# Local scores of two heads in one product: k laid block-diagonally, in a fused attention and expert kernel

## The chip, the cores and the metric

The kernel runs on one core of a Trainium2 chip. The metric is device time in microseconds (us) for one execution of the whole program. Before the change, three runs took 709.04, 709.7 and 718.24 us; their median, 709.7 us, is the time before.

## The reference

The program computes an attention over 8 batches of 8 heads, 576 tokens and 64 dimensions, and feeds its output to a layer of 8 experts, of which each token takes one.

```python
# attention: a pooled part and a local part
q_d, k_d, v_d = (x.reshape(B, H, S // 4, 4, D).mean(axis=3) for x in (q, k, v))
out_up = np.repeat(sm_attn(q_d, k_d, v_d), 4, axis=2)
mask = np.abs(pos[:, None] - pos[None, :]) < 4
scores = np.where(mask, scale * np.matmul(q, k.transpose(0, 1, 3, 2)), -1e9)
attn = softmax(scores)
x = out_up + np.matmul(attn, v)
# experts: each token goes to the best of 8
e_idx = np.argmax(x @ w_gate + modality_bias[modality_id], axis=1)
out[mask_e] = gate_w * (np.maximum(x[mask_e] @ w1[e], 0) @ w2[e])
```

Here `sm_attn` is a scaled softmax attention, and the local part lets a query see only the keys less than four positions away.

## The kernel before, in words

**Steps.** The attention stage runs 32 steps; step n takes two heads of one batch, so four steps make a batch. q and k of two steps are loaded with one load each (`load_qk`, three buffers), transposed on TensorE into PSUM (`tp`, L274, and `tpt`, L287, which serves two steps), and copied by ScalarE to SBUF (`qT`, L292 and L294; `kT_`, L300 and L302). In SBUF the 128 partitions of `qT2` and `kT2` hold the 64 dimensions of the first head and then the 64 of the second. Both have two halves, for even and odd steps. For the part of k in `kT0`, one copy moves 512 columns of all 128 partitions; `kT1`, in even steps only, copies 64 columns for each of two steps, in one instruction.

**Local scores.** A step's 576 queries are cut into 24 blocks of 24, four to each of 6 groups of 96. A block needs 32 keys (a window of 24 with three on either side, and two more). `mk` (L328) first writes the mask into a PSUM tile of 128 x 6 x 32 by a product with the identity; `sc` (L337) then adds 24 products of 64 rows, 24 stationary columns (q) and 32 moving columns (k), each at a tile position of 64 rows and 32 columns. There are two such tiles a step, `sc0` for the first head and `sc1` for the second. VectorE takes the maximum (`lm`, L344) and subtracts it (`le`, L350), ScalarE exponentiates (L355), VectorE sums (`z`, L381) and inverts (`zr`, L387), GpSimd scales (`nl`, L391), VectorE transposes 32 x 32 blocks (`lt`, L402), ScalarE copies them into the zeroed `Pw` (L407), and TensorE multiplies with v (`avl`, L442).

**Pooled scores.** GpSimd adds groups of four tokens in two instructions each: `qe` and `d` (L308, `halves`) and `qd` and `kd` (L312, `whole`). Then come the products `scd` (L364), the maximum `dm` (L369), the exponentials `de` (L377), scaling on GpSimd (`nd`, L395), transposes on TensorE (`pdt`, L413), copies by ScalarE (`PdT`, L420), products with the pooled v (`vp`, L262; `avd`, L427) and `Od` (L432). VectorE adds both parts into `X` (L453). GpSimd also issues the scatters of the routing table (L599).

**What sets the order.** All of this is emitted in an order written out by hand. `PHASE` gives each operation a phase in units of a step; operation p of step n is placed at n + p, and the sorted list is the order of every engine's in-order queue. Within a step of the steady state the order on TensorE is: transposes of q and k, `mk0`, (`tpt`), `sc1` of the step before, (`vp`), `avd`, `scd`, `avl`, `sc0`, `pdt`, `mk1`. On ScalarE it is: `qT0`, `kT0`, three of four `Pw` copies, (`qT1`), `Od`, (`kT1`), the exponential, the last `Pw` copy, three `de`, two `PdT`. SP issues the loads in the same sorted order.

**Buffers.** PSUM tiles come from three tags: "T" (three buffers: `tp`, `tpt`, `vp`, `pdt`), "S" (three: `sc`, `scd`) and "A" (two: `avd`, `avl`, the router's). A tile waits until the reader of the one three (or two) allocations earlier has finished.

**Experts.** From about 260 us on, the experts' products run with both operands split in two float32 parts (L886, L934).

Of the kernel before, what the change touches and what calls it, by code (L numbers as in the profile page):

```python
# [7 lines left out]
F32 = mybir.dt.float32  # L8
F32R = mybir.dt.float32r
BF16 = mybir.dt.bfloat16  # L10
I32 = mybir.dt.int32
AF = mybir.ActivationFunctionType
ALU = mybir.AluOpType
# [4 lines left out]
B, H, S, D = 8, 8, 576, 64  # L18
# [4 lines left out]
SUB, WIN = 24, 32  # L23
BLK = 4 * SUB
NB = 6
PAD = 3
KT = S - SUB + WIN
QS = 1.0 / 128
NEG = -8.0e9 * QS
# [17 lines left out]
TB, SB = 3, 3  # L47
# [30 lines left out]
class Consts:  # L78
    def __init__(s, tc, pool, psum):
        nc = tc.nc  # L80

        s.ps = psum
        pool.tile([128, 48], F32, name="pad")
        s.dummy = pool.tile([128, 128], BF16, name="dummy")
        nc.vector.memset(s.dummy, 0.0)
        s.busy(nc, 12)
        s.ident = pool.tile([128, 128], F32, name="ident")
        make_identity(nc, s.ident)
        s.identb = pool.tile([128, 128], BF16, name="identb")
        make_identity(nc, s.identb)  # L90

        x = pool.tile([128, 1], F32, name="warm")
        nc.vector.memset(x, 0.0)
        nc.scalar.activation(x, x, AF.Exp)
        m = pool.tile([128, WIN], BF16, name="band")
        nc.gpsimd.memset(m, 0.0)
        for j in range(4):
            t = m[32 * j : 32 * j + 32]
            nc.gpsimd.affine_select(out=t, in_=t, pattern=[[1, WIN]], compare_op=ALU.is_ge, fill=NEG, base=0,
                                    channel_multiplier=-1)  # L100
            nc.gpsimd.affine_select(out=t, in_=t, pattern=[[-1, WIN]], compare_op=ALU.is_ge, fill=NEG, base=6,
                                    channel_multiplier=1)
        s.mask = pool.tile([128, NB, WIN], BF16, name="mask")
        nc.vector.tensor_copy(s.mask, m.unsqueeze(1).broadcast_to([128, NB, WIN]))
        nc.vector.memset(s.mask[0:32, 0, 0:PAD], NEG)
        nc.vector.memset(s.mask[96:128, NB - 1, SUB + PAD : WIN], NEG)

        s.pool = pool.tile([128, 32], F32, name="pool")

# [18 lines left out]
    def load(s, tc, pool, work, rows, mid, bias, w_gate):  # L128
        nc = tc.nc
        s.wg = pool.tile([128, 4, 32], F32, name="wg")  # L130
        nc.vector.memset(s.wg, 0.0)
        for f in range(2):
            for a in range(2):
                nc.sync.dma_start(s.wg[64 * a : 64 * a + 64, 2 * f : 2 * f + 2, 0:NE],
                                  w_gate[256 * f + 128 * a : 256 * f + 128 * a + 128].rearrange("(g d) e -> d g e", g=2))
        s.mi = rows.tile([128, 2 * DM], F32, name="R", bufs=NR)[:36, :256].bitcast(I32)
        nc.sync.dma_start(s.mi, mid.bitcast(I32).rearrange("(t x) -> t x", t=36))
        s.bb = work.tile([128, 2, NE], F32, name="bb")
        nc.sync.dma_start(s.bb, bias.unsqueeze(0).broadcast_to([128, 2, NE]))
# [53 lines left out]
class Attention:  # L193


    def __init__(s, tc, ctx, ectx, C, psum, q, k, v):
        s.tc, s.C, s.ps = tc, C, psum
        nc = s.nc = tc.nc
        s.q, s.k, s.v = q, k, v

        s.ld = ectx.enter_context(tc.tile_pool(name="ald", bufs=2, side="right", reuse_waits="tile"))
        s.wk = ctx.enter_context(tc.tile_pool(name="awk", bufs=2, reuse_waits="tile"))
        s.one = ctx.enter_context(tc.tile_pool(name="aone", bufs=1, reuse_waits="tile"))
        s.QK, s.t = {}, {}
        s.vw = [(s.ld, s.one)[j].tile([128, H * NB, D], F32, name=f"vw{j}", bufs=1) for j in range(2)]

        s.qT2 = s.ld.tile([128, 2, S], F32, name="qT", bufs=1)
        s.kT2 = s.ld.tile([128, 2, KT], F32, name="kT", bufs=1)
        nc.vector.memset(s.kT2[:, :, 0:PAD], 0.0)
        nc.vector.memset(s.kT2[:, :, S + PAD :], 0.0)  # L210
        s.Pw = [s.one.tile([128, 2 * NB, 4, SUB], F32, name=f"Pw{j}") for j in range(NPW)]

        s.De = [s.one.tile([128, 3, 32 * NB], F32, name=f"de{j}") for j in range(3)]
        for j in range(2):
            nc.vector.memset(s.vw[j][0:32, 0], 0.0)
            nc.vector.memset(s.vw[j][96:128, H * NB - 1], 0.0)

        for j in range(3):
            nc.vector.memset(s.De[j], 0.0)
# [49 lines left out]
    def tp(s, n, nm):  # L269

        src = s.QK[n // 2]["qk".index(nm)]
        p = s.t["tp", nm, n] = s.ps.tile([128, 512], F32, name="tp", tag="T", bufs=TB)
        for j in range(4):
            s.nc.tensor.transpose(p[:, 128 * j : 128 * j + 128],  # L274
                                  src[:, 5 * (n % 2) + j].rearrange("p a d -> p (a d)"), s.C.ident)
# [7 lines left out]
    def tpt(s, n, i):  # L283

        p = s.t["tp", "t"] = s.ps.tile([128, 2, 128], F32, name="tpt", tag="T", bufs=TB)
        for x in range(2):
            s.nc.tensor.transpose(p[:, x], s.QK[n // 2][x][:, 4].rearrange("p a d -> p (a d)"), s.C.ident)  # L287
# [7 lines left out]

    def kT_(s, n, i):
        g = n % 2
        if i:
            t = s.kT2.rearrange("m g t -> m (g t)")[:, PAD + 512 : PAD + 512 + 2 * (KT - 512)]
            s.nc.scalar.copy(t.rearrange("m (g t) -> m g t", g=2)[:, :, :64], s.t["tp", "t"][:, 1].rearrange("m (g t) -> m g t", g=2))  # L300
        else:
            s.nc.scalar.copy(s.kT2[:, g, PAD + 64 * g : PAD + 64 * g + 512], s.t.pop(("tp", "k", n)))  # L302

    def halves(s, nm, n, T):

        d2 = s.t[nm, n] = s.ld.tile([128, 144, 2], F32, name=nm, bufs=1)
        T4 = T.rearrange("m (g t) -> m g t", t=4)
        s.nc.gpsimd.tensor_tensor(d2, T4[:, :, 0:2], T4[:, :, 2:4], op=ALU.add)  # L308

    def whole(s, nm, n, d2):  # L310
        dd = s.t[nm, n] = s.ld.tile([128, 144], F32, name=nm)
        s.nc.gpsimd.tensor_tensor(dd, d2[:, :, 0], d2[:, :, 1], op=ALU.add)  # L312

    def qe(s, n, i):
        s.halves("qe", n, s.qT2[:, n % 2])

    def qd(s, n, i):
        s.whole("qd", n, s.t.pop(("qe", n)))

    def d(s, n, i):  # L320
        s.halves("d", n, s.kT2[:, n % 2, PAD : PAD + S])

    def kd(s, n, i):
        s.whole("kd", n, s.t.pop(("d", n)))

    def mk(s, n, a):
        p = s.t["sc", n, a] = s.ps.tile([128, NB, WIN], F32, name="sc", tag="S", bufs=SB)
        s.nc.tensor.matmul(p, s.C.identb, s.C.mask, start=True, stop=False, skip_group_check=True)  # L328

    def sc(s, n, a):  # L330

        p, qT, kT = s.t["sc", n, a], s.qT2[:, n % 2], s.kT2[:, n % 2]
        r = slice(64 * a, 64 * a + 64)
        for i in range(NB):
            for j in range(4):
                q0 = BLK * i + SUB * j
                s.nc.tensor.matmul(p[32 * j : 32 * j + SUB, i, :], qT[r, q0 : q0 + SUB], kT[r, q0 : q0 + WIN],  # L337
                                   start=False, stop=(i == NB - 1), skip_group_check=True,
                                   tile_position=(64 * a, 32 * j))

    def lm(s, n, a):
        if ("lm", n) not in s.t:
# [91 lines left out]
    def avl(s, n, i):  # L434

        b, hp = divmod(n, 4)
        vw, Pw = s.vw[b % 2], s.Pw[n % NPW]
        p = s.t["avl", n, i] = s.ps.tile([128, 3, BLK], F32, name="avl", tag="A", bufs=2)
        for c in range(3):
            for a in range(2):  # L440
                k = 3 * i + c
                s.nc.tensor.matmul(p[64 * a : 64 * a + 64, c], vw[:, NB * (4 * (hp // 2) + hp % 2 + 2 * a) + k, :],  # L442
                                   Pw[:, NB * a + k], start=True, stop=True, skip_group_check=True)

    def X(s, n, i, dst):

# [782 lines left out]
```

## Time and profile before

| | |
|---|---|
| median of three runs | 709.7 us |
| the profiled execution | 716.96 us |
| its span, first to last instruction | 715.3 us |
| granted TensorE clock, mean | 0.974 |
| attention's scores, first to last | 7.5 to 257.5 us |
| TensorE busy | 662.0 us, 93% |
| VectorE, ScalarE, GpSimd busy | 379.2, 358.7, 262.9 us |

The profile is one execution on the chip. PE is TensorE's products, PEld its weight loads, DVE VectorE, ACT ScalarE, POOL GpSimd, SP the queue that issues loads; L337 is line 337 of the kernel. A row of the groups tells the line, engine, operation, output and input tiles, shape, count, then the busy time (overlaps counted once) and the mean duration of one, and after the second bar the idle time of the engine just before these instructions, with what ended it. "issue" is time in which an engine waited for nothing that the profile shows. A float32 product has two records in the trace. In a row such as 64*24 64x32, 64 rows and 24 stationary columns are used, and the moving operand has 32 columns.

### The profile page before, as it was taken

The numbers are of one execution on the slowest core, as the hardware profiler recorded it, in microseconds if no ns is written. First come the engines' busy times: TensorE is split into PE (matmuls) and PEld (weight loads), VectorE is DVE, ScalarE is ACT, GpSimd is POOL, SyncE is SP. The second block draws the span as 40 slices with busy tenths as digits, with TensorE's granted clock in tenths as the row PEclk, the third lists the DMA queues.
The fourth block names the chain that finished last, engine by engine and source line by source line (L and its number), as shares of the span: only waits on it lengthen the run. The fifth ranks groups of instructions, "written<-read, shape, count | busy, mean of one in ns | idle before, by whom it ended". The sixth has DMA issues, their size and how long they took to land. (4 is left out here: it accounts for less than half of the span.)

```text
span 715.3 us, 19216 instructions
## 1 busy us (share of the span) xinstructions
PE 662.0 (93%) x7467; PEld 535.7 (75%) x7467; DVE 379.2 (53%) x877; ACT 358.7 (50%) x804; POOL 262.9 (37%) x351
## 2 busy tenths in 40 slices
PE   7889999998968798999999999999999999999991
PEld 4677776776746666887888888888888888889790
DVE  3678687787848686836533245333453243525510
ACT  3678777777756574534444234433444234444610
POOL 6756665857647857353030310403103011010200
PEclk9799999999989899999999999999999999999996
DMA  9799799897889757579560744516435154346400
GB/s 178 148 186 173 162 165 181 174 184 130 145 147 214 152 151 186 154 228 294 143 219 21 189 148 116 179 58 190 165 102 156 67 162 148 103 133 186 159 13 29
DMA packets 179439, 107.93 MB, mean 151 GB/s; under 512 B 139309, under 2 KB 157777, under 8 KB 179346
## 3 DMA queue, kind: packets, MB, share of 16 engines
q1 hardware_dynamic: 172274, 87.49, 53.1%
q0 software_dynamic: 7072, 19.18, 8.3%
q8 instruction: 60, 0.98, 0.7%
q14 instruction: 33, 0.27, 0.2%
HBM read 87.39 MB, written 19.51 MB: 149 GB/s over the span
## 5 line engine op out<-in xcount | busy, mean ns | idle before, releaser
L938 POOL DMA_INDIRECT out_dram<-o,tg x37 | 40.9, 1106 | 302.7 <-ACT o L937 245.5
L817 DVE TENSOR_TENSOR wlo<-raw,whi 128x1024 fp32r<-128x1024 f32 x73 | 87.4, 1222 | 84.4 <-ACT whi L811 74.4
L891 DVE SCALAR_TENSOR_TENSOR hl<-l,hh 128x512 fp32r<-128x512 f32 x72 | 49.4, 688 | 101.7 <-ACT hh L890 101.7
L934 PE MATMUL l<-whi,hh 128*128 128x512 f32 x256 | 100.2, 395 | 0.0
L934 PE MATMUL l<-wlo,hh 128*128 128x512 f32 x256 | 99.6, 390 | 0.0
L934 PE MATMUL l<-whi,hl 128*128 128x512 f32 x256 | 99.6, 390 | 0.0
L890 ACT ACTIVATE hh<-l 128x512 fp32r<-128x512 f32 x72 | 42.9, 597 | 110.7 <-PE l L886 109.3
L886 PE MATMUL l<-xh,whi 128*128 128x512 f32 (+1 forms) x256 | 95.0, 374 | 0.4 <-DVE hl L891 0.2
L886 PE MATMUL l<-xh,wlo 128*128 128x512 f32 (+1 forms) x256 | 94.8, 370 | 0.0
L886 PE MATMUL l<-xl,whi 128*128 128x512 f32 (+1 forms) x256 | 94.7, 370 | 0.0
L811 ACT CAST whi<-raw 128x1024 fp32r<-128x1024 f32 x70 | 71.4, 1050 | 28.2 <-DMA raw<-in_moe_w_dram 18.2
L937 ACT ACTIVATE o<-l,tg 128x512 f32<-128x512 f32 x37 | 25.3, 687 | 98.5 <-PE l L934 70.5
L407 ACT COPY Pw<-lt 32x288 f32<-32x288 f32 x128 | 54.6, 426 | 3.2 <-DVE lt L402 1.8
L934 PEld LDWEIGHTS l<-wlo,hh 128*128 128x128 f32 x256 | 48.1, 188 | 10.1
L886 PEld LDWEIGHTS l<-xh,whi 128*128 128x128 f32 x256 | 48.1, 188 | 9.7 <-POOL xg L1063 0.5
L934 PEld LDWEIGHTS l<-whi,hl 128*128 128x128 f32 x256 | 48.1, 188 | 9.5
L934 PEld LDWEIGHTS l<-whi,hh 128*128 128x128 f32 x256 | 48.1, 188 | 9.5
L886 PEld LDWEIGHTS l<-xh,wlo 128*128 128x128 f32 x256 | 48.3, 189 | 8.3
L886 PEld LDWEIGHTS l<-xl,whi 128*128 128x128 f32 x256 | 48.3, 189 | 8.0
L337 PE MATMUL sc<-kT,qT 64*24 64x32 f32 x3072 | 45.5, 195 | 8.1 <-issue 7.4
L391 POOL TENSOR_TENSOR le<-le,zr 128x384 f32<-128x384 f32 x32 | 26.8, 836 | 70.0 <-DVE zr L387 53.5
L337 PEld LDWEIGHTS sc<-kT,qT 64*24 64x24 f32 x3072 | 35.3, 101 | 22.8 <-issue 18.2
(241 smaller groups left out, 1277.9 us busy)
## 6 DMA issues: line engine op xcount, KB each, us to landing
raw<-in_moe_w_dram SPq DMA_DIRECT2D x176, 128.0 KB
raw<-in_moe_w_dram SPq DMA_DIRECT2D x44, 512.0 KB
vw<-in_v_dram SPq DMA_DIRECT2D x53, 192.0 KB
qt<-in_q_dram SPq DMA_DIRECT2D x30, 288.0 KB
kt<-in_k_dram SPq DMA_DIRECT2D x30, 288.0 KB
xs<-R SPq DMA_DIRECT2D x64, 128.0 KB
vw<-in_v_dram SPq DMA_DIRECT2D x15, 96.0 KB
xs<-R SPq DMA_DIRECT2D x12, 64.0 KB
```

Source lines behind the costliest of these rows:

```text
L337: s.nc.tensor.matmul(p[32 * j : 32 * j + SUB, i, :], qT[r, q0 : q0 + SUB], kT[r, q0 : q0 + WIN], start=False, stop=(i == NB - 1), skip_gro ...
L391: s.nc.gpsimd.tensor_tensor(e, e, z[:, : 2 * NB].unsqueeze(2).broadcast_to([128, 2 * NB, WIN]), op=ALU.mult)
L407: s.nc.scalar.copy(s.Pw[n % NPW][r, :, j, :SUB], s.t["lt", n][r, :, :SUB])
L811: (nc.gpsimd.tensor_copy if turn <= 4 else nc.scalar.copy)(hi, raw)
L817: (nc.gpsimd if turn == 4 else nc.vector).tensor_tensor(lo, raw, hi.bitcast(F32), op=ALU.subtract)
L886: nc.tensor.matmul(p[:, f % n, :], a[:, fs], x[:, k, :N], start=(k == 0 and i == 0), stop=(k == 3 and i == 2))
L890: nc.scalar.activation(hh[:, g, :N], p, AF.Relu)
L891: nc.vector.scalar_tensor_tensor(hl[:, g, :N], p, 0.0, hh[:, g, :N].bitcast(F32), op0=ALU.max, op1=ALU.subtract)
L934: nc.tensor.matmul(p, a[:, f, hs], x[:, f % 2, :], start=(f == 0 and i == 0), stop=(f == 7 and i == 2))
L937: nc.scalar.mul(o, p, T[:, h, 1:2].bitcast(F32))
L938: nc.gpsimd.indirect_dma_start(out=s.out[:, :], out_offset=bass.IndirectOffsetOnAxis(ap=T[:, h, 0:1], axis=0), in_=o, in_offset=None, boun ...
```

## The change

`kT2` (128 x 2 x 584 columns, for even and odd steps) becomes `kB` (128 x 2 x 2 x 584): each step now has two column sections, the first with the first head's k in partitions 0 to 63, the second with the second head's in partitions 64 to 127; the rest is zero, cleared once at the start. A product of 128 rows with the stacked q and a window out of both sections then gives 32 columns for each head, 64 together. So a group `sc` has 12 products (128 rows, 24 stationary and 64 moving columns, tile positions of 128 rows and 32 columns) in place of 24; `sc0` takes the first three blocks of 96 queries of both heads, and `sc1` the last three. The masks follow: the first tile's excludes the keys before the sequence, the second's those after it, and a second mask tile is made. ScalarE makes the copies of k by halves: two in place of one for `kT0`, four in place of one for `kT1`. The halving `d` of k on GpSimd reads the two sections with two instructions of 64 partitions in place of one of 128. `avl` reads `Pw` in the new order of blocks and heads. `PHASE` and everything else stay as they are.

```diff
-        nc.vector.memset(s.mask[0:32, 0, 0:PAD], NEG)
-        nc.vector.memset(s.mask[96:128, NB - 1, SUB + PAD : WIN], NEG)
+        nc.vector.memset(s.mask[0:32, 0:2, 0:PAD], NEG)
+        s.band = m
...
-        s.kT2 = s.ld.tile([128, 2, KT], F32, name="kT", bufs=1)
-        nc.vector.memset(s.kT2[:, :, 0:PAD], 0.0)
-        nc.vector.memset(s.kT2[:, :, S + PAD :], 0.0)
+        s.kB = s.ld.tile([128, 2, 2, KT], F32, name="kT", bufs=1)
+        nc.vector.memset(s.kB, 0.0)
+        s.mask = s.one.tile([128, NB, WIN], BF16, name="mask")
+        nc.vector.tensor_copy(s.mask, C.band.unsqueeze(1).broadcast_to([128, NB, WIN]))
+        nc.vector.memset(s.mask[96:128, NB - 2 :, SUB + PAD : WIN], NEG)
...
     def kT_(s, n, i):
         g = n % 2
-        if i:
-            t = s.kT2.rearrange("m g t -> m (g t)")[:, PAD + 512 : PAD + 512 + 2 * (KT - 512)]
-            s.nc.scalar.copy(t.rearrange("m (g t) -> m g t", g=2)[:, :, :64], s.t["tp", "t"][:, 1].rearrange("m (g t) -> m g t", g=2))
-        else:
-            s.nc.scalar.copy(s.kT2[:, g, PAD + 64 * g : PAD + 64 * g + 512], s.t.pop(("tp", "k", n)))
+        p = s.t["tp", "t"][:, 1] if i else s.t.pop(("tp", "k", n))
+        for a in range(2):
+            r = slice(64 * a, 64 * a + 64)
+            if i:
+                t = s.kB[r].rearrange("m g a t -> m g (a t)")[:, :, KT * a + PAD : KT * a + PAD + 512 + 64]
+                s.nc.scalar.copy(t[:, 0, 512:], p[r, :64])
+                s.nc.scalar.copy(t[:, 1, :64], p[r, 64:])
+            else:
+                s.nc.scalar.copy(s.kB[r, g, a, PAD + 64 * g : PAD + 64 * g + 512], p[r])
 
     def halves(s, nm, n, T):
...
-        T4 = T.rearrange("m (g t) -> m g t", t=4)
-        s.nc.gpsimd.tensor_tensor(d2, T4[:, :, 0:2], T4[:, :, 2:4], op=ALU.add)
+        for t, x in T:
+            T4 = x.rearrange("m (g t) -> m g t", t=4)
+            s.nc.gpsimd.tensor_tensor(d2[t], T4[:, :, 0:2], T4[:, :, 2:4], op=ALU.add)
...
     def d(s, n, i):
-        s.halves("d", n, s.kT2[:, n % 2, PAD : PAD + S])
+        r = [slice(64 * a, 64 * a + 64) for a in range(2)]
+        s.halves("d", n, [(r[a], s.kB[r[a], n % 2, a, PAD : PAD + S]) for a in range(2)])
...
-    def sc(s, n, a):
-
-        p, qT, kT = s.t["sc", n, a], s.qT2[:, n % 2], s.kT2[:, n % 2]
-        r = slice(64 * a, 64 * a + 64)
-        for i in range(NB):
+    def sc(s, n, x):
+
+        p, qT, kB = s.t["sc", n, x], s.qT2[:, n % 2], s.kB[:, n % 2]
+        for i in range(NB // 2):
             for j in range(4):
-                q0 = BLK * i + SUB * j
-                s.nc.tensor.matmul(p[32 * j : 32 * j + SUB, i, :], qT[r, q0 : q0 + SUB], kT[r, q0 : q0 + WIN],
-                                   start=False, stop=(i == NB - 1), skip_group_check=True,
-                                   tile_position=(64 * a, 32 * j))
+                q0 = BLK * (NB // 2 * x + i) + SUB * j
+                s.nc.tensor.matmul(p[32 * j : 32 * j + SUB, 2 * i : 2 * i + 2, :], qT[:, q0 : q0 + SUB],
+                                   kB[:, :, q0 : q0 + WIN], start=False, stop=(i == NB // 2 - 1),
+                                   skip_group_check=True, tile_position=(0, 32 * j))
...
-                                   Pw[:, NB * a + k], start=True, stop=True, skip_group_check=True)
+                                   Pw[:, 2 * k + a], start=True, stop=True, skip_group_check=True)
```

More of the change, by code (lines that the diff above doesn't have):

```diff
@@ L314, in qe @@
     def qe(s, n, i):
-        s.halves("qe", n, s.qT2[:, n % 2])
+        s.halves("qe", n, [(slice(0, 128), s.qT2[:, n % 2])])
     def qd(s, n, i):
@@ L320, in d, with mk @@
     def d(s, n, i):
-        s.halves("d", n, s.kT2[:, n % 2, PAD : PAD + S])
+        r = [slice(64 * a, 64 * a + 64) for a in range(2)]
+        s.halves("d", n, [(r[a], s.kB[r[a], n % 2, a, PAD : PAD + S]) for a in range(2)])
     def kd(s, n, i):
         s.whole("kd", n, s.t.pop(("d", n)))
-    def mk(s, n, a):
-        p = s.t["sc", n, a] = s.ps.tile([128, NB, WIN], F32, name="sc", tag="S", bufs=SB)
-        s.nc.tensor.matmul(p, s.C.identb, s.C.mask, start=True, stop=False, skip_group_check=True)
-    def sc(s, n, a):
-        p, qT, kT = s.t["sc", n, a], s.qT2[:, n % 2], s.kT2[:, n % 2]
-        r = slice(64 * a, 64 * a + 64)
-        for i in range(NB):
+    def mk(s, n, x):
+        p = s.t["sc", n, x] = s.ps.tile([128, NB, WIN], F32, name="sc", tag="S", bufs=SB)
+        s.nc.tensor.matmul(p, s.C.identb, s.mask if x else s.C.mask, start=True, stop=False, skip_group_check=True)
+    def sc(s, n, x):
+        p, qT, kB = s.t["sc", n, x], s.qT2[:, n % 2], s.kB[:, n % 2]
+        for i in range(NB // 2):
             for j in range(4):
-                q0 = BLK * i + SUB * j
-                s.nc.tensor.matmul(p[32 * j : 32 * j + SUB, i, :], qT[r, q0 : q0 + SUB], kT[r, q0 : q0 + WIN],
-                                   start=False, stop=(i == NB - 1), skip_group_check=True,
-                                   tile_position=(64 * a, 32 * j))
+                q0 = BLK * (NB // 2 * x + i) + SUB * j
+                s.nc.tensor.matmul(p[32 * j : 32 * j + SUB, 2 * i : 2 * i + 2, :], qT[:, q0 : q0 + SUB],
+                                   kB[:, :, q0 : q0 + WIN], start=False, stop=(i == NB // 2 - 1),
+                                   skip_group_check=True, tile_position=(0, 32 * j))
     def lm(s, n, a):
```

## The prediction

> **What bounds the kernel now.** I read the page first, then the busy time by stretches.
>
> ```profile
> span 715.3 us, 19216 instructions
> PE 662.0 (93%) x7467; PEld 535.7 (75%) x7467; DVE 379.2 (53%) x877; ACT 358.7 (50%) x804; POOL 262.9 (37%) x351
> ...
> q8 instruction: 60, 0.98, 0.7%
> ```
> ```profile
> core 0: us, PE busy (x) PEld busy (x) DVE busy (x) ACT busy (x) POOL busy (x), PEclk, DMA share, GB/s
> 45.00:195.00 150.00, 138.41 (x3333) 107.81 (x3331) 117.06 (x372) 115.39 (x351) 97.62 (x142) 1.00 0.87 167
> 300.00:715.00 415.00, 397.70 (x1903) 332.60 (x1901) 164.52 (x225) 156.57 (x215) 75.48 (x69) 0.98 0.46 138
> ```
> TensorE is busy nearly everywhere, but only the attention stage runs the changed code; from 300 us on the expert products fill TensorE (397.7 of 415 us), and what attention saves or loses simply moves them. In the stretch from 45 to 195 us TensorE is the fullest (138 of 150), ScalarE stands at 77%, VectorE at 78%, GpSimd at 65%, DMA at 0.87. The 20 copies of k counted below make this stretch 20 steps of 7.5 us. So TensorE leads, and three others have little room.
>
> Next, the group of local scores within a step, on TensorE:
>
> ```profile
> 66.61 0.60 PE L337 MATMUL sc<-kT,qT 64*24 64x32 f32 x48
> 67.15 0.86 PE L413 MATMUL pdt<-ident,de 128*96 128x128 f32 x6
> ...
> 68.98 0.75 PE L337 MATMUL sc<-kT,qT 64*24 64x32 f32 x43
> 70.24 0.27 PE L337 MATMUL sc<-kT,qT 64*24 64x32 f32 x5 [0.50 <-issue]
> 70.44 0.71 PE L427 MATMUL avd<-PdT,vd 96*64 96x144 f32 x8
> 71.08 0.95 PE L364 MATMUL scd<-kd,qd 64*64 64x144 f32 x12
> 71.96 1.21 PE L442 MATMUL avl<-Pw,vw 128*64 128x96 f32 x24
> ...
> 77.26 1.06 PE L262 MATMUL vp<-vw,pool 128*32 128x256 f32 x12
> ```
> ```profile
> L337 PE MATMUL sc<-kT,qT 64*24 64x32 f32 x3072 | 45.5, 195 | 8.1 <-issue 7.4 <-ACT kT L302 0.4
> L442 PE MATMUL avl<-Pw,vw 128*64 128x96 f32 x768 | 39.4, 251 | 2.5 <-issue 1.3 <-ACT Pw L407 1.1
> L262 PE MATMUL vp<-vw,pool 128*32 128x256 f32 x192 | 18.9, 414 | 3.2 <-DMA vw<-in_v_dram 3.2
> L302 ACT COPY kT<-tp 128x512 f32<-128x512 f32 x32 | 18.7, 584 | 4.0 <-PE tp L274 3.9
> L300 ACT COPY kT<-tpt 128x128 f32<-128x128 f32 x16 | 4.2, 263 | 0.0
> L308 POOL TENSOR_TENSOR d<-kT 128x288 f32<-128x288 f32 x32 | 21.4, 668 | 2.4 <-ACT kT L300 2.3
> L407 ACT COPY Pw<-lt 32x288 f32<-32x288 f32 x128 | 54.6, 426 | 3.2 <-DVE lt L402 1.8
> L420 ACT COPY PdT<-pdt 96x288 f32<-96x288 f32 x64 | 22.5, 396 | 13.6 <-PE pdt L413 5.9 <-remote 4.6 <-PE tp L274 2.7
> ```
> The reader is to see two things. A product has two records, so a group of 24 products is x48; undisturbed it takes 0.60 us. And some groups break off after 43 records with nothing to wait for ("issue"): at 68.98 the group needs 1.53 us. Over 64 groups, 45.5 us busy and 7.4 us idle stand against 64 x 0.60 = 38.4 us: 14.5 us of broken flow (a little of it at half clock).
>
> **The change, part by part.** *TensorE.* The rows give a rule for such groups: records of N columns take about (records - tiles) x N x 0.87 ns / tiles, plus one record's duration; the 0.87 is the slope between 195 ns at 32 columns and 251 ns at 96. It gives (24 - 2) x 96 x 0.87 / 2 + 251 = 1.17 us for avl (measured 1.21) and (12 - 3) x 256 x 0.87 / 3 + 414 = 1.08 us for vp (1.06), so products of 128 rows overlap in column tiles as well. For the old score group it gives (48 - 4) x 32 x 0.87 / 4 + 195 = 0.50 us, 0.10 under the measured 0.60. The new group is 24 records of 64 columns on four tiles: (24 - 4) x 64 x 0.87 / 4 + 223 = 0.50 us. The columns streamed are the same; only the instructions halve. I take the 0.10 as the feeding of 48 weight loads and 48 products, which 24 of each don't need: 64 x 0.10 = **6.4 us** off (bounds 0 and 6.4). Of the 14.5 us of broken flow I take **10 us** off (bounds 0 and 14.5): the break comes at record 43 of 48, so a group of 24 ends before the point at which these ran dry, while the program still has to be fetched (60 instruction DMAs by the page, which I take to be what breaks the flow; no row ties the two) and a break may fall elsewhere. TensorE together: 16.4 us, bounds 0 and 20.9. The mask products stay two a step.
>
> By the Trainium skill, TensorE: Matmul & The Clock Gate, section "Wait — 56ns, not 53.3ns?", starts of two matmuls are never less than about 25 ns apart however small N is; 48 of them would then be 1.2 us and 24 of them 0.6, a gain of 38 us. The trace disagrees: 48 records lie in 0.60 us, under 12.5 ns each.
>
> *ScalarE.* The big copy of k becomes two of 64 rows and 512 columns. Rows don't shorten a copy: 32 x 288 takes 426 ns and 96 x 288 takes 396. So each is 584 ns: + 0.584 x 32 = 18.7 us. The small copy (every second step) becomes four of 64 columns. The line through 263 ns at 128 columns and 584 at 512 gives 210 ns at 64: 4 x 210 - 263 = 577 ns, x 16 = 9.2 us. Together **27.9 us** more on ScalarE, 0.87 a step (if short ones cost as little as half, 23). What covers it is ScalarE's idle time:
>
> ```profile
> L377 ACT ACTIVATE de<-scd,dm 128x144 f32<-128x144 f32 x58 | 21.4, 377 | 3.7 <-DVE dm L369 2.7 <-DVE w L529 0.4
> L420 ACT COPY PdT<-pdt 96x288 f32<-96x288 f32 x40 | 13.9, 396 | 6.8 <-PE pdt L413 3.8 <-PE tp L274 2.7 <-ACT de L377 0.2
> L294 ACT ACTIVATE qT<-tp 128x512 f32<-128x512 f32 x20 | 12.0, 599 | 4.8 <-PE tp L274 4.1 <-POOL d L308 0.5 <-issue 0.2
> L302 ACT COPY kT<-tp 128x512 f32<-128x512 f32 x20 | 11.7, 584 | 0.1
> L432 ACT ACTIVATE Od<-avd 128x144 f32<-128x144 f32 x20 | 5.8, 291 | 11.1 <-PE avd L427 7.3 <-issue 2.5 <-PE scd L364 1.1
> ```
> These are the 20 steps from 45 to 195 us. ScalarE works 115.4 us there; with 20 x 0.87 = 17.4 it works 132.8. TensorE, by its own saving, could do the stretch in 150 - 16.4 x 20/32 = 139.8 us. ScalarE would then have 7 us of idle time left where it has 35 now, and its order is fixed: the copies of k stand ahead of the three Pw copies, of Od (which frees the PSUM buffer of the second avl), of the exponentials and of PdT. PdT empties the buffer that the next transpose of k fills, and the second half of the scores in kT1 must be there before sc0. Of its waits, those on TensorE (qT, Od, PdT) shrink when ScalarE is late, since their producers run ahead; the rest need not. I take it that **half of TensorE's 16.4 us** is lost to ScalarE: 8.2 us (bounds 0 and, without any cover, 27.9).
>
> *GpSimd.* The first halving of k (d) becomes two instructions on 64 rows. No row shows GpSimd on 64 rows at this size; bounds are half of 668 ns each (nothing added) and 668 each, 21.4 us over 32 steps. I take the upper one, since ScalarE's rows don't go by rows either. It is covered by the 52 us that GpSimd idles in the 150, except where scatters crowd it:
>
> ```profile
> 94.54 0.83 POOL L391 TENSOR_TENSOR le<-le,zr 128x384 f32<-128x384 f32 x1 [6.94 <-ACT qT L292]
> ...
> 98.55 0.67 POOL L308 TENSOR_TENSOR d<-kT 128x288 f32<-128x288 f32 x1
> ...
> 104.04 0.93 POOL L395 TENSOR_TENSOR de<-de,zr 128x432 f32<-128x432 f32 x1
> ```
> ```profile
> 105.02 0.86 PE L413 MATMUL pdt<-ident,de 128*96 128x128 f32 x6 [0.28 <-POOL de L395]
> ```
> From 94.5 to 105 us GpSimd runs without a pause, and TensorE waits for its de. One d lies in that run, so the wait grows by 0.67 us; if six of the eight batches have such a run, which is my choice, that is **4.0 us** (bounds 0 and 10). Uncovered, all of it would be 21.4.
>
> *Start.* The block-diagonal tile is cleared whole, 2336 columns on VectorE, some 2.2 us, and the first scores wait for 1.2 us more of copies. I cost both at nothing: TensorE stops for data right after, and these waits absorb them.
>
> ```profile
> 15.72 1.08 PE L274 MATMUL tp<-ident,kt 128*128 128x128 f32 x4 [3.47 <-DMA kt<-in_k_dram]
> 19.97 1.50 PE L262 MATMUL vp<-vw,pool 128*32 128x256 f32 x9 [1.80 <-DMA vw<-in_v_dram]
> ```
> ```profile
> L219 DVE MEMSET de<- 128x576 f32 x3 | 1.6, 538 | 0.3 <-issue 0.2
> ```
> The 2.2 is 2336 / 576 x 538 ns. Without the cover of the loads both would be about 3 us. The second mask (0.2 us of VectorE) and the new order of blocks cost nothing: maxima, exponentials and transposes work on tiles of the same shape.
>
> **Sum:** -6.4 - 10 + 8.2 + 4.0 = -4.2 us. The profiled execution took 716.96 us (span 715.3, 1.7 around it), so it would be 712.8; that execution lies 7.3 over the median of the runs shown, 709.7, and on the median the forecast is **705.5 us**.
>
> **Rivals.** *ScalarE's copies are hidden after all*: its 35 us of waits all sit opposite TensorE and vanish. For: 132.8 is under 139.8. Against: the fixed order. Then -16.4, with or without the 4: 693.3 to 697.3.
>
> *The group goes by the number of instructions, not by columns*: 24 records take half of 0.60, 0.30 us, which saves 19.2, and all 14.5 of the broken flow goes. TensorE would gain 33.7, but ScalarE's 132.8 us of work holds the 150 us stretch to a gain of 17.2, 27.5 over 32 steps: 682. Against: avl and vp follow the columns. The skill's 25 ns, named above, would be such a count.
>
> *ScalarE becomes the bound and keeps its waits* (the other side): the waits before qT, Od and PdT stay whole, 4.8 + 11.1 + 6.8 = 22.7 us, because TensorE, held back by late PdT and kT1, brings tp, avd and pdt late as well. The stretch is then 115.4 + 17.4 + 22.7 = 155.5 us, 5.5 more, 8.8 over 32 steps; with GpSimd's 4.0, 722.5. It decides from the point where more than 17.2 of the 35 us stay. For: the loop PdT, transpose, copy, scores, pdt closes in every step. Against: tp and avd need nothing else from ScalarE early.
>
> *The wide products don't run four at a time*: 24 x 64 x 0.87 ns + 223 = 1.56 us a group, 61 us more, 771. Against: vp.
>
> **How the numbers follow.** Chances: forecast 0.50, copies hidden 0.17, by instructions 0.06, ScalarE with its waits 0.24, not four at a time 0.03. The range **691 to 724 us** reaches the hidden copies on one side (less 2 for the unknown rest of the broken flow) and the slow rival on the other. Of the measurable, a change of 2% (14 us, about what a measurement of this kernel can tell from none) is 695.5 or 723.9: the hidden copies land under it in two cases of three and the instruction rival always, faster **0.18**; the slow rival lands over it in about half of its cases, and the last one always, slower **0.16**; same **0.66**.
>
> **What would show it.** Right: score groups x24 of about 0.50 us with almost no "issue" ahead of their records; ScalarE's k copies x64 at 0.58 us and its busy time up by about 28 us; in the steady stretch its idle time down from 35 us per 20 steps to under 20, and new TensorE waits for ACT kT, Od or PdT; d x64 at 0.67 us. Wrong: groups that still break off (then no gain is left), TensorE waits for ScalarE as small as now with shorter steps (hidden), or steps over 7.5 us with ScalarE's waits as before (the slow rival).

## The result, and the profile after

The changed kernel takes **743.3 us** (median of five runs, 738.01 to 745.7) against 709.7 for the kernel before, measured beside it (five runs, 709.04 to 718.24). The ratio is 1.0457, 95% interval 1.0411 to 1.0502: 4.6% slower, outside the predicted range. (Ratios are taken over undisturbed runs, so they are not always the quotient of the medians.)

The page of the changed kernel's profiled execution, which took 738.01 us, answers to the first fence of the prediction, and its busy time by stretches to the second:

```profile
span 736.3 us, 16297 instructions
PE 660.7 (90%) x5931; PEld 531.1 (72%) x5931; DVE 384.0 (52%) x877; ACT 381.5 (52%) x884; POOL 281.2 (38%) x383
...
q8 instruction: 48, 0.79, 0.6%
```
```profile
core 0: us, PE busy (x) PEld busy (x) DVE busy (x) ACT busy (x) POOL busy (x), PEclk, DMA share, GB/s
45.00:195.00 150.00, 121.30 (x2086) 92.59 (x2087) 103.48 (x322) 111.34 (x348) 95.72 (x142) 0.94 0.88 161
300.00:715.00 415.00, 411.43 (x1977) 343.79 (x1976) 181.47 (x270) 167.52 (x230) 77.51 (x73) 1.00 0.49 149
```
From 45 to 195 us every compute engine does less than before: TensorE 121.3 us (138.4 before), VectorE 103.5 (117.1), ScalarE 111.3 (115.4), GpSimd 95.7 (97.6). Nothing became the bound by its work; the steps became longer, and all four engines wait for one another. Where the loss arose can be read from the last score groups (the header of this view of a tile is: count, shortest, median and longest in ns, first and last start):

```profile
L344 PE MATMUL sc<-kT,qT x54: 219/219/238, 259.8 to 271.9; 128*24 128x64 f32 x54
L344 PE MATMUL sc<-kT,qT x48: 219/219/238, 276.4 to 278.6; 128*24 128x64 f32 x48
```
The last one starts at 278.6 us, at 257.5 before: 21.1 us later, and the span is 21.0 us longer. All of the loss that these two traces show is in the attention stage. It is less than the 33.6 us between the medians, since the profiled execution before lies 7.3 us over its median and the one after 5.3 us under.

TensorE's rows of one step in time, to be held against the prediction's from 66.61 on:

```profile
67.58 0.54 PE L344 MATMUL sc<-kT,qT 128*24 128x64 f32 x24
68.05 0.71 PE L434 MATMUL avd<-PdT,vd 96*64 96x144 f32 x8
71.93 0.95 PE L371 MATMUL scd<-kd,qd 64*64 64x144 f32 x12 [3.17 <-POOL kd L319]
72.82 2.14 PE L449 MATMUL avl<-Pw,vw 128*64 128x96 f32 x24
```
The score groups are what was forecast: 24 records in 0.54 us, unbroken. But the pooled scores now stand still for 3.17 us for kd from GpSimd. They then take their 0.95 us as before, and the group behind them, avl, takes 2.14 us where it took 1.21: from 72.9 to 76.2 us the granted clock was 0.50. The reason for the pause is one engine further on. GpSimd's rows before, and then of the changed kernel, at the same place in the order:

```profile
64.92 1.18 POOL L599 DMA_INDIRECT tab<-ig,si  x1 [0.17 <-issue]
...
68.12 0.67 POOL L308 TENSOR_TENSOR d<-kT 128x288 f32<-128x288 f32 x1
68.94 1.00 POOL L599 DMA_INDIRECT tab<-ig,si  x1 [0.15 <-issue]
69.97 0.44 POOL L312 TENSOR_TENSOR kd<-d 128x144 f32<-128x144 f32 x1
```
```profile
62.37 0.83 POOL L398 TENSOR_TENSOR le<-le,zr 128x384 f32<-128x384 f32 x1 [5.18 <-DVE zr L394]
63.38 1.18 POOL L606 DMA_INDIRECT tab<-ig,si  x1 [0.17 <-issue]
...
66.58 0.66 POOL L315 TENSOR_TENSOR d<-kT 64x288 f32<-64x288 f32 x1
69.45 0.66 POOL L315 TENSOR_TENSOR d<-kT 64x288 f32<-64x288 f32 x1 [2.21 <-DMA tab<-ig,si]
70.39 1.00 POOL L606 DMA_INDIRECT tab<-ig,si  x1 [0.28 <-POOL d L315]
71.46 0.42 POOL L319 TENSOR_TENSOR kd<-d 128x144 f32<-128x144 f32 x1
71.84 0.83 POOL L398 TENSOR_TENSOR le<-le,zr 128x384 f32<-128x384 f32 x1
...
78.94 0.66 POOL L315 TENSOR_TENSOR d<-kT 64x288 f32<-64x288 f32 x1 [2.43 <-DMA tab<-ig,si]
```
The two halves of d do not follow one another. The first runs at 66.58; the second, on partitions 64 to 127, waits until the scatter of the routing table (`tab`), issued at 63.38, has landed: it starts 6.07 us after the scatter. While it waits, GpSimd's queue stands still, and kd and the scaling of the local weights (`nl`, whose tile the trace names le) come late. The scatter has nothing to do with k. In the kernel before, d starts 3.2 us after a scatter and does not wait for it. The wait belongs to the program as it was built: in its list of waits the second d names the scatters issued since the last one; the first names none, and neither does the whole d of the kernel before. The traces agree. They record the instructions that wait on a semaphore in a queue, at d's line 42 of them in the changed kernel and one before (the line also holds qe):

```profile
L315 POOLq EVENT_SEMAPHORE  x42: 17/43/4757, 8.1 to 273.8; - x42
```
```profile
L308 POOLq EVENT_SEMAPHORE  x1: 17/17/17, 7.7 to 7.7; - x1
```

The groups of the changed kernel show how far the wait goes:

```profile
L344 PE MATMUL sc<-kT,qT 128*24 128x64 f32 x1536 | 36.8, 231 | 1.0 <-ACT kT L308 1.0
L371 PE MATMUL scd<-kd,qd 64*64 64x144 f32 x384 | 33.2, 309 | 26.1 <-POOL kd L319 24.7 <-POOL pool L112 1.3
L308 ACT COPY kT<-tp 64x512 f32<-64x512 f32 x64 | 36.9, 577 | 1.0 <-PE tp L276 0.3
L306 ACT COPY kT<-tpt 64x64 f32<-64x64 f32 x32 | 6.8, 212 | 1.5 <-POOL d L315 1.5
L305 ACT COPY kT<-tpt 64x64 f32<-64x64 f32 x32 | 6.5, 203 | 0.4
L315 POOL TENSOR_TENSOR d<-kT 64x288 f32<-64x288 f32 x64 | 42.4, 662 | 38.5 <-DMA tab<-ig,si 32.6 <-ACT kT L306 4.1 <-ACT qT L296 0.5
L409 DVE STREAM_TRANSPOSE lt<-le 128x384 f32<-128x384 f32 x32 | 18.3, 573 | 46.5 <-POOL le L398 46.5
L414 ACT COPY Pw<-lt 32x288 f32<-32x288 f32 x128 | 54.7, 427 | 30.1 <-DVE lt L409 17.1 <-issue 11.6
```
Rows of the kernel before that the prediction does not show:

```profile
L364 PE MATMUL scd<-kd,qd 64*64 64x144 f32 x384 | 31.2, 296 | 0.4 <-POOL pool L112 0.4
L402 DVE STREAM_TRANSPOSE lt<-le 128x384 f32<-128x384 f32 x32 | 18.2, 568 | 1.4 <-POOL le L391 1.4
L391 POOL TENSOR_TENSOR le<-le,zr 128x384 f32<-128x384 f32 x32 | 26.8, 836 | 70.0 <-DVE zr L387 53.5 <-ACT qT L292 10.5 <-ACT qT L294 2.9
L413 PE MATMUL pdt<-ident,de 128*96 128x128 f32 x192 | 28.9, 288 | 5.3 <-POOL de L395 5.2
```
In the changed kernel GpSimd waits 32.6 us for scatters in front of d, in 14 waits. TensorE waits 26.1 us in front of scd (0.4 before), VectorE 46.5 in front of lt (1.4 before), ScalarE 30.1 in front of Pw (3.2 before). The groups avl are busy for 45.0 us in the changed kernel and for 39.4 before, which the granted clock (0.94 from 45 to 195 us, 1.00 before) would explain at least in part; no experiment separates this share.

### The profile page after: what moved, and what is told of

It reads as the page before. It is cut to its first block, busy times and chain, and to the rows that moved or that the text cites. A ratio compares the mean times of both kernels' runs of the same rounds, so it can differ in the third digit from the quotient of the medians.

```text
span 736.3 us, 16297 instructions
## 1 busy us (share of the span) xinstructions
PE 660.7 (90%) x5931; PEld 531.1 (72%) x5931; DVE 384.0 (52%) x877; ACT 381.5 (52%) x884; POOL 281.2 (38%) x383
## 5 line engine op out<-in xcount | busy, mean ns | idle before, releaser
L944 ACT ACTIVATE o<-l,tg 128x512 f32<-128x512 f32 x37 | 25.4, 687 | 97.6 <-PE l L941 63.7
L414 ACT COPY Pw<-lt 32x288 f32<-32x288 f32 x128 | 54.7, 427 | 30.1 <-DVE lt L409 17.1
L315 POOL TENSOR_TENSOR d<-kT 64x288 f32<-64x288 f32 x64 | 42.4, 662 | 38.5 <-DMA tab<-ig,si 32.6
L371 PE MATMUL scd<-kd,qd 64*64 64x144 f32 x384 | 33.2, 309 | 26.1 <-POOL kd L319 24.7
L371 PEld LDWEIGHTS scd<-kd,qd 64*64 64x64 f32 x384 | 23.7, 141 | 33.8 <-POOL kd L319 29.2
```

Source lines behind the costliest of these rows:

```text
L315: s.nc.gpsimd.tensor_tensor(d2[t], T4[:, :, 0:2], T4[:, :, 2:4], op=ALU.add)
L371: s.nc.tensor.matmul(p[r, c, :], qd[r, 40 * c : 40 * c + 64], kd[r, :], start=True, stop=True, skip_group_check=True)
L414: s.nc.scalar.copy(s.Pw[n % NPW][r, :, j, :SUB], s.t["lt", n][r, :, :SUB])
L944: nc.scalar.mul(o, p, T[:, h, 1:2].bitcast(F32))
```

## The experiments

Several theories stood against each other, all made after the result. Mine (W): the wait that the second d carries makes the loss. The rivals: ScalarE's added copies (S), GpSimd's added time (G), and the wide products themselves.

### One part alone: d in two halves

The kernel before, with only this (and with `halves` running over the two parts, as in the change):

```diff
...
     def d(s, n, i):
-        s.halves("d", n, s.kT2[:, n % 2, PAD : PAD + S])
+        r = [slice(64 * a, 64 * a + 64) for a in range(2)]
+        s.halves("d", n, [(x, s.kT2[x, n % 2, PAD : PAD + S]) for x in r])
```

> The kernel before, with GpSimd's first halving of k (d) alone split in two instructions of 64 partitions; scores, copies and masks as before. Theory W (the second of the two instructions waits until the scatters issued since the last d have landed, so GpSimd stands still and kd, scd and le come late): most of the loss is here, 25 to 38 us over the kernel before, with d waiting on the scatters for about 30 us in all. Theory S (ScalarE's extra copies are the bound): at most 4 us over. Theory G (only GpSimd's extra 21 us of work counts): 5 to 15 us over, without waits on scatters.

Measured: 739.99 us, the kernel before beside it 712.23; ratio 1.0388 (1.0299 to 1.0476). The row of d:

```profile
L309 POOL TENSOR_TENSOR d<-kT 64x288 f32<-64x288 f32 x64 | 42.4, 662 | 43.7 <-DMA tab<-ig,si 41.9 <-DMA xg<-xs,tg 0.8
```
With k stored as before, narrow products and ScalarE's old copies, this edit alone brings 27.6 us (3.88% of 712.23) and the same wait, at 41.9 us longer than the 30 or so expected. The intervals of this run and of the whole change overlap.

### One part alone: ScalarE's copies by halves

The kernel before, with two 64-partition copies for `kT0` and four for `kT1` into the old `kT2`:

```diff
...
+                s.nc.scalar.copy(t[:, PAD + 512 : PAD + 576], p[r, :64])
+                s.nc.scalar.copy(t[:, KT + PAD : KT + PAD + 64], p[r, 64:])
...
+                s.nc.scalar.copy(s.kT2[r, g, PAD + 64 * g : PAD + 64 * g + 512], p[r])
```

> The kernel before, with ScalarE's copies of k alone split (two of 64 partitions for one of 512 columns, four of 64 columns for one of 128), into the old tile. ScalarE's busy time should rise by some 23 to 28 us. Theory W: 0 to 8 us over the kernel before. Theory S: 25 us or more over.

Measured: 715.74 us beside 712.23; ratio 1.0023 (0.996 to 1.0086). ScalarE's copies stand in the profile as in the changed kernel:

```profile
L306 ACT COPY kT<-tp 64x512 f32<-64x512 f32 x64 | 36.9, 577 | 3.1 <-PE tp L274 2.1
```
ScalarE is busy 381.7 us, 23.0 more than the 358.7 before, and the time does not move measurably. The copies are not the cause.

### The change without the wait: d's second half on VectorE

```diff
-        for t, x in T:
+        for e, (t, x) in zip((s.nc.gpsimd, s.nc.vector), T):
...
-            s.nc.gpsimd.tensor_tensor(d2[t], T4[:, :, 0:2], T4[:, :, 2:4], op=ALU.add)
+            e.tensor_tensor(d2[t], T4[:, :, 0:2], T4[:, :, 2:4], op=ALU.add)
```

> The changed kernel, with the second half of d on VectorE, so that GpSimd has no second instruction and no wait on the scatters; ScalarE's copies and the wide products stay. Theory W: 695 to 712 us, the loss is gone. Theory S: 735 us or more. Theory G: 695 to 712 as well.

Measured: 710.77 us beside 712.23; ratio 0.9984 (0.9945 to 1.0023). The loss is gone, though not turned into a gain. This alone does not separate the wait from GpSimd's added time, since both are gone; a later experiment does. Three of its groups:

```profile
L319 POOL TENSOR_TENSOR kd<-d 128x144 f32<-128x144 f32 x32 | 14.6, 455 | 37.2 <-DVE d L315 36.4
L398 POOL TENSOR_TENSOR le<-le,zr 128x384 f32<-128x384 f32 x32 | 26.7, 835 | 29.9 <-DVE zr L394 22.3 <-ACT Od L439 3.1 <-ACT kT L305 2.9
L409 DVE STREAM_TRANSPOSE lt<-le 128x384 f32<-128x384 f32 x32 | 18.3, 572 | 6.5 <-POOL le L398 6.2
```
kd now waits 36.4 us for VectorE's half, more than the 32.6 that d waited for scatters in the changed kernel, and yet VectorE waits only 6.5 us for the local weights (le, written by `nl`). In front of nl GpSimd's own wait fell to 29.9 us; in the kernel before that row has 70.0. So kd's wait stands in steps in which GpSimd would have waited for zr a moment later in any case. The wait for scatters stands in the steps that carry scatters. There the kernel before leaves GpSimd no pause: from the scatter at 64.92 on, the first of over a microsecond is the 2.87 us in front of `nl` at 83.64. What it loses there VectorE, ScalarE and TensorE lose too (46.5 us in front of lt).

### The wide products alone

One copy of all 128 partitions into section 0, and d whole from section 0. The second head's scores then take zeros for keys, which leaves a part of the computation out; `kT1` too is one copy again.

```diff
...
+            s.nc.scalar.copy(s.kB[:, g, 0, PAD + 64 * g : PAD + 64 * g + 512], s.t.pop(("tp", "k", n)))
...
+        s.halves("d", n, [(slice(0, 128), s.kB[:, n % 2, 0, PAD : PAD + S])])
```

> The wide products alone: ScalarE copies k with one instruction each into the first section of the block-diagonal tile, and d is one instruction that reads it, so copies and GpSimd cost what they cost before; the second head's scores take zeros for keys, which leaves part of the computation out. All theories: TensorE's own gain, which I put at 16 us: 690 to 700 us. If the products of 128 rows gain nothing, 707 to 712.

Measured: 704.23 us beside 712.23; ratio 0.9915 (0.9877 to 0.9952), 6 us, where all theories had 16. Two rows of its groups and the last of its scores:

```profile
L341 PE MATMUL sc<-kT,qT 128*24 128x64 f32 x1536 | 35.5, 224 | 0.5 <-ACT kT L306 0.4
L417 PE MATMUL pdt<-ident,de 128*96 128x128 f32 x192 | 28.8, 288 | 19.2 <-POOL de L399 19.0
```
```profile
L341 PE MATMUL sc<-kT,qT x96: 219/219/238, 226.8 to 242.0; 128*24 128x64 f32 x96
```
The score groups cost 36.0 us, busy and idle, where the row before has 53.6 (45.5 and 8.1; of the idle time the prediction counted the 7.4 of "issue"): 17.6 freed. But in front of pdt TensorE now waits 19.2 us, nearly all for GpSimd's de, 13.9 more than in the trace before. The last score group starts at 242.0 us, 15.5 earlier than in the trace before. That is more than the 6 us of the ratio, since the two profiled executions differ by 14.4 us (716.96 and 702.52) and the one before lies 7.3 over its median. The products bring a gain, and it is smaller than these two traces show.

### GpSimd's time without the wait

The kernel before, with a second d of all 128 partitions into a tile that nobody reads:

```diff
...
+        if nm == "d":
+            x2 = s.ld.tile([128, 144, 2], F32, name="dx", bufs=1)
+            s.nc.gpsimd.tensor_tensor(x2, T4[:, :, 0:2], T4[:, :, 2:4], op=ALU.add)
```

> The kernel before, with a second instruction of GpSimd per step that halves k again (all 128 partitions, into a scratch tile that nothing reads), 0.67 us each: GpSimd's extra time without the split by partitions, and without a wait on the scatters. Theory W (the wait on the scatters makes the loss): 0 to 8 us over the kernel before. Theory G (GpSimd's time makes it): 15 us or more over.

Measured: 714.78 us beside 712.57; ratio 1.0046 (1.0009 to 1.0083), 3.3 us. The first of the two instructions:

```profile
L308 POOL TENSOR_TENSOR d<-kT 128x288 f32<-128x288 f32 x32 | 22.3, 696 | 0.3 <-ACT kT L302 0.3
```
GpSimd's added time alone costs a tenth of the whole loss. No wait of d on a scatter appears.

### The scatters moved away from d

The changed kernel with four of the five scatters of a batch moved in the order, to right behind d or kd, so that almost a step passes until the next d (those of the last two batches stay where they were):

```diff
...
-    "R4": 7.7000, "gt": 7.8318, "pr": 7.8428, "pl": 7.9316, "st4": 9.0000, "W2": 8.5000, "R1": 8.2990, "W0": 9.1000,
-    "st2": 8.5946, "st0": 8.7485, "R2": 9.2990, "st3": 9.5946, "st1": 10.2000, "R3": 10.2990, "W1": 11.1000,
+    "R4": 7.7000, "gt": 7.8318, "pr": 7.8428, "pl": 7.9316, "st4": 8.8600, "W2": 8.5000, "R1": 8.2990, "W0": 9.1000,
+    "st2": 9.7485, "st0": 8.7485, "R2": 9.2990, "st3": 9.8600, "st1": 10.7485, "R3": 10.2990, "W1": 11.1000,
```

> The changed kernel with only the phases of the router's scatters moved, so that each is issued just behind a d or a kd, in place of just ahead of the exponentials' scaling. GpSimd does the same work and the second d still waits for scatters issued since the last d, but these have then had most of a step (some 7 us) to land, where they took 5.9 to 6.9 us. Theory W: most of the loss goes, 705 to 722 us, and d's waits on the scatters fall from 33 us to under 10. Theory G or S: no change, 735 to 745.

Measured: 725.1 us beside 712.57; ratio 1.0144 (1.0065 to 1.0223). The loss falls from 4.6% to 1.4%, with d still in halves. Both expectations were too bold: the time lies over the 722 us given, and some half of the wait for `tab` is left, not under 10 us:

```profile
L315 POOL TENSOR_TENSOR d<-kT 64x288 f32<-64x288 f32 x64 | 42.4, 663 | 34.9 <-DMA tab<-ig,si 18.3 <-DMA xg<-xs,tg 5.3 <-ACT Pw L414 4.0
```
The edit changes the phases of the scatters alone, but the place of the first expert steps is computed from the last of these phases, so they come about half a step later as well. With this reservation, that the time falls with the wait is a second sign that the wait is the loss. A part of the wait is now for the gathers of the expert stage (`xg`, 5.3 us), which are software DMAs as well.

### The change with d whole

As in the wide products alone, d reads the first section only, so the second head's pooled keys are zero and a part of the computation is left out.

```diff
-        s.halves("d", n, [(r[a], s.kB[r[a], n % 2, a, PAD : PAD + S]) for a in range(2)])
+        s.halves("d", n, [(slice(0, 128), s.kB[:, n % 2, 0, PAD : PAD + S])])
```

> The changed kernel with d as one instruction of 128 partitions that reads the first section alone (the second head's pooled keys are then zero, which leaves part of the computation out): wide products and ScalarE's copies, nothing of GpSimd's part. Against the wide products alone (704 us, 8 under the kernel before) it tells what ScalarE's copies cost once the products are wide: theory W with hidden copies 702 to 707; with half of the gain lost to ScalarE, as I forecast, 707 to 713.

Measured: 707.12 us beside 712.57; ratio 0.9958 (0.9917 to 0.9999). Wide products and ScalarE's added copies, with one instruction on GpSimd: the 4.6% are gone. Against the wide products alone (0.9915) the copies cost 0.43%, some 3 us; the two ratios were measured on different occasions, and their intervals overlap. The time lies on the border of the two ranges expected.

```profile
L315 POOL TENSOR_TENSOR d<-kT 128x288 f32<-128x288 f32 x32 | 21.3, 665 | 0.0
```

### VectorE's half, and two small copies

The version with the second half on VectorE, with a tile view that lets ScalarE copy `kT1` in two instructions of 64 partitions and 2 x 64 columns, not four:

```diff
...
-                s.nc.scalar.copy(t[:, 0, 512:], p[r, :64])
-                s.nc.scalar.copy(t[:, 1, :64], p[r, 64:])
+                t = s.kF[r, o : o + 2 * (2 * KT - 512)].rearrange("m (g t) -> m g t", g=2)[:, :, :64]
+                s.nc.scalar.copy(t, p[r].rearrange("m (g t) -> m g t", g=2))
```

> A version that might beat both: the changed kernel with the second half of d on VectorE and the four small copies made as two (one per head, both steps in one instruction of 64 x 128 columns, 0.26 us). ScalarE saves about 0.3 us in every second step against the run with d on VectorE (710.8 us): 704 to 710 us, if ScalarE still holds the steps; 709 to 712 if it does not.

Measured: 710.4 us; ratio 0.9979 (0.9946 to 1.0013), the same as with four copies (0.9984). Nothing gained: those copies were no limit.

### Two instructions cut by tokens

The kernel before, d in two instructions of all 128 partitions and half the tokens each:

```diff
...
+        for x in (slice(0, 72), slice(72, 144)) if nm == "d" else (slice(0, 144),):
+            s.nc.gpsimd.tensor_tensor(d2[:, x], T4[:, x, 0:2], T4[:, x, 2:4], op=ALU.add)
```

> The kernel before, with d in two instructions on all 128 partitions, half of the tokens each, into the same tile: as many instructions as in the changed kernel, cut by columns in place of partitions. If it is the cut by partitions that brings the wait on the scatters (theory W, narrowed): no wait of d on scatters, and 0 to 4 us over the kernel before. If two writes to one tile bring it: 25 us or more over.

Measured: 709.48 us beside 708.16; ratio 1.0008 (0.9969 to 1.0048).

```profile
L309 POOL TENSOR_TENSOR d<-kT 128x144 f32<-128x144 f32 x64 | 25.9, 425 | 0.0
L338 PE MATMUL sc<-kT,qT 64*24 64x32 f32 x3072 | 42.1, 195 | 4.4 <-issue 3.7 <-ACT kT L302 0.4
```
Sixty-four instructions as in the first experiment, without idle time in front of any. So it is not that d is two instructions that write one tile; it is the cut by partitions. What about this cut brings the wait is not separated: the waiting half comes second, works on other partitions than the first, and is the one on partitions 64 to 127, and no run exchanges the two halves.

### Each section whole, on 128 partitions

The changed kernel, d and kd once for each section, each on all 128 partitions (half of them zero), four instructions in place of three. `scd` takes its rows from the two results, and the small copies are made as two:

```diff
...
+            s.halves(f"d{'ab'[a]}", n, [(slice(0, 128), s.kB[:, n % 2, a, PAD : PAD + S])])
...
+        for x in "ab":
+            s.whole("kd" + x, n, s.t.pop(("d" + x, n)))
```

> The changed kernel with the halving and the sum of k (d, kd) made once per section on all 128 partitions, so GpSimd has two instructions more per step (0.67 + 0.43 us) than the kernel before but none on part of the partitions; the small copies made as two. The result is the reference's. Theory W, narrowed: no wait on the scatters, 708 to 718 us, GpSimd's extra time costing 2 to 8 us over the run with d whole (707). If GpSimd's time counts more than the earlier run with d twice showed: 720 or more.

Measured: 710.29 us beside 708.16; ratio 1.0046 (1.0018 to 1.0073). It computes all that the changed kernel does, with more work on GpSimd, and loses 0.5%, not 4.6.

```profile
L316 POOL TENSOR_TENSOR da<-kT 128x288 f32<-128x288 f32 x32 | 21.3, 667 | 0.0
```

### VectorE's half earlier

As the version with two small copies, with VectorE's half of d placed at phase 0.65 in place of 0.7407, ahead of work that it stood behind:

```diff
...
-    "kT1": 0.5356, "sc0": 0.5591, "qe": 0.6232, "qd": 0.6242, "lm0": 0.7343, "d": 0.7407, "le0": 0.8414, "kd": 0.8569,
+    "kT1": 0.5356, "sc0": 0.5591, "qe": 0.6232, "qd": 0.6242, "lm0": 0.7343, "d0": 0.7407, "d1": 0.6500, "le0": 0.8414, "kd": 0.8569,
```

> A version that might beat both: d's second half on VectorE, placed ahead of X and of the first maximum in VectorE's order in place of behind them, and the small copies made as two. In the run with d on VectorE, kd waited for VectorE's half for some 30 us, and GpSimd's de then came late to pdt (11 us on TensorE). If that held the steps: 703 to 708 us, and kd's waits fall under 10 us. If not: 709 to 712, and if X comes late by it, more.

Measured: 711.2 us beside 708.16; ratio 1.0056 (1.0026 to 1.0087).

```profile
L320 POOL TENSOR_TENSOR kd<-d 128x144 f32<-128x144 f32 x32 | 13.7, 428 | 17.6 <-DVE d L334 16.0
L403 POOL TENSOR_TENSOR le<-le,zr 128x384 f32<-128x384 f32 x32 | 26.7, 834 | 48.9 <-DVE zr L399 35.9 <-ACT LT L508 5.4 <-ACT Od L444 4.1
```
The wait in front of kd falls from 37.2 to 17.6 us, the one in front of nl rises from 29.9 to 48.9, and the time does not fall. The attempt failed (kd's waits were to come under 10 us, the time to 703 to 708), and it supports the reading above: what GpSimd waits for kd in these steps was slack. No version that computes all of the attention beat the kernel before.

## Why the prediction was wrong, point by point

**The step that failed** is GpSimd's: d was costed as time only ("21.4 us over 32 steps", of which 4.0 uncovered, with "bounds 0 and 10"), and the wait that the second instruction carries was left out. Its own time was sized well: 662 ns on 64 partitions (668 forecast, by the upper bound), and 3.3 us on the path when it comes without the wait, against a forecast of 4.0 (near by luck in part, since the six batches in it were a choice). But with the halves on two sets of partitions the same edit costs 27.6 us. The prediction saw the scatters ("except where scatters crowd it") and took them as crowding only. The cover it named, GpSimd's 52 us of idle time, is a sum over steps: it lies in front of nl before and after a batch's scatters, and the steps between, in which the new wait stands, have little of it.

**TensorE** was right in kind. The group has 24 records in 0.54 us (0.50 forecast), almost no "issue" is left ahead of them, and the columns, not the instructions, set its length. 17.6 us were freed against 16.4 forecast, if the two profiled executions are compared. Measured in time, the wide products bring 6: this term of the sum was sized too large by some 10 us. One reason may be that the broken flow differs between executions. The five traces with the old groups have 53.6 (the kernel before), 54.9 (copies by halves), 52.5 (d twice), 46.5 (cut by tokens) and 44.6 us (d in halves), busy and idle; the forecast took its 10 us from one of the three with more breaks. That explains a part at most. Another reason may be the longer wait for de (13.9 us); no experiment took that wait away, so its share is open.

**ScalarE**: the durations were right (577 ns for 64 x 512 against 584; 203 and 212 for 64 x 64 against 210), and the rows of the copies add up to 27.3 us more (36.9 + 6.8 + 6.5 against 18.7 + 4.2); ScalarE's busy time, in which overlaps count once, rose by 22.8. "Half of TensorE's 16.4 us", 8.2, was too much: the copies cost 0.2% alone and some 3 us beside the wide products. ScalarE's rows in the 20 steps from 45 to 215 us, after:

```profile
L414 ACT COPY Pw<-lt 32x288 f32<-32x288 f32 x79 | 33.7, 427 | 19.3 <-DVE lt L409 11.5 <-issue 6.9
L427 ACT COPY PdT<-pdt 96x288 f32<-96x288 f32 x38 | 13.1, 397 | 5.5 <-PE pdt L420 5.3
L439 ACT ACTIVATE Od<-avd 128x144 f32<-128x144 f32 x20 | 5.8, 288 | 0.2
```
The wait in front of Od went from 11.1 us to 0.2 and that of PdT from 6.8 to 5.5. With d whole, where no wait for scatters stretches the steps, they are 0.3 and 2.2 from 45 to 215 us: ScalarE's cover was there. In the changed kernel its new wait is Pw's, behind lt and so behind GpSimd.

**The start** cost nothing, as forecast; the first scores come at 7.8 us (7.5 before).

**The slow rival** came out on the right side for a wrong reason. It had ScalarE keep its waits on TensorE, and the largest of them, in front of Od, vanished. None of the rivals named GpSimd's queue. Without the wait the terms as measured, -6 for the products, +3 for the copies and +3.3 for GpSimd, come to about nothing. That this is near the forecast of -4.2 is luck: the gain and ScalarE's share of the loss were both forecast too large (16.4 and 8.2). The ratios with d whole (0.9958) and with each section on 128 partitions (1.0046) lie on either side of one.

**What stays open** is why the second instruction carries the wait. The Trainium skill, GPSIMD Engine Reference, section "2.1 Instruction dispatch", says that each of GpSimd's cores serves 16 partitions and that an instruction reading partitions which another core wrote in the preceding one must wait on that one's completion. The second d reads nothing that the first one wrote, so this does not by itself ask for a wait; that a cut by partitions is a case in which waits are put in as a precaution is a guess. The runs agree with it so far as cuts by tokens or by section have no wait and cuts by partitions have one. The section does not speak of scatters that are still in flight, and no run here shows why they are among what is waited for. It is also open why TensorE's saving in the changed kernel left no trace in its time: the whole change is no faster than the old products with d in halves (1.0457 against 1.0388, overlapping). It is not that TensorE waited longer for kd: in front of scd it waited 26.1 us in the changed kernel and 29.2 with d in halves and the old products.

```profile
L366 PE MATMUL scd<-kd,qd 64*64 64x144 f32 x384 | 34.5, 318 | 29.2 <-POOL kd L313 28.1 <-POOL pool L112 1.1
```

## What to carry to other kernels

An instruction cut in two is not two half-priced instructions: look up what each one waits for, and what its engine has in flight: here a software DMA issued by GpSimd came to stand in front of GpSimd's own arithmetic. Cutting by columns with all partitions, or giving the halves to two engines (GpSimd kept partitions 0 to 63), avoided it here. And idle time covers a new wait only if it lies in the same steps: read it step by step, not as a sum over a stretch.

## What was not expected of the hardware

- GpSimd's add takes as long on 64 partitions as on 128 (662 against 668 ns at 288 elements), while half the elements take 425 ns.
- A scatter on GpSimd's queue took 6.07 us until the instruction that waited for it started (63.38 to 69.45), and 6.11 the next time (72.83 to 78.94), though its own record is about 1 us long.
- The granted clock fell around TensorE's pauses: 0.94 from 45 to 195 us, 1.00 before. At 0.50 (72.9 to 76.2 us, about 1 us behind a pause of 3.17) the group avl took 2.14 us where it takes 1.21 otherwise.
- Half as many products of double width removed the breaks in TensorE's flow almost entirely (7.4 us of "issue" to under 0.5), and the program's instruction DMAs fell from 60 to 48.
